# Units of 256 tokens by eight heads in a fused RWKV-6 and HyperMixer kernel: two tokens a partition, decay products on transposed operands, order from a list schedule

## Chip, cores, metric

One core of a Trainium2 chip. The time is device time of one execution in microseconds. Runs are marked fast or slow; on one core a run is called slow when it took over 1.5% more than the fastest of the same kernel. Comparisons below use fast runs unless the text says otherwise.

## The reference, cut

```python
# r, k, v, w: (4 batches, 8 heads, 768 tokens, 48); u: (8, 48)
for t in range(S):                                    # RWKV-6 with a decay of its own per channel
    cur = einsum('bhd,bhe->bhde', u * k[t], v[t])
    y[t] = einsum('bhd,bhde->bhe', r[t], state + cur)
    state = w[t][..., None] * state + einsum('bhd,bhe->bhde', k[t], v[t])
x = y as (4, 768, 384)                                # then a token MLP of each batch
wq, wk = x @ w_q, x @ w_k                             # 384 -> 64
mixed = (wq @ wk.T / 8) @ x
out = relu(mixed) @ w_out
```

Both kernels work in chunks of 128 tokens: within a chunk a masked product A of decayed r and k, across chunks a state SB of 48 x 48 a head; after that the MLP of a batch, which needs all its tokens. Decays are cumulated as logarithms with a triangular matmul (`cw`) and come back through Exp.

## The kernel before

Each of 16 preparations (`prep`) loads two heads over all 768 tokens of one batch. The decays go on in the natural layout, the products are transposed after that, and the diagonal term u*k*r is made in f32 on GpSimd and summed on VectorE. No order is given: the framework takes the program's.

```python
def prep(b, hp, AmB, RKT, VB, Vd, ptp):
    for ap, tl in ((w, wG), (k, kG), (r, rG), (v, vG)):
        nc.sync.dma_start(out=tl, in_=ap[b, ds(hp * 2, 2)].rearrange(
            "h (c p) d -> p (h c) d", p=C))               # packets of 192 bytes
    # ... Ln, two cw matmuls, Exp(+) to ecwx, Exp(-) to emcw ...
    nc.vector.tensor_tensor(pad(Rd), chd(rG), ecwx..., ALU.mult)
    nc.gpsimd.tensor_tensor(pad(Kd), chd(kG), emcw..., ALU.mult)     # KdS
    for c in range(NCH): mm(psT[:, 0, ds(c * C, C)], Rd[:, c], ID128, trans=True)
    for c in range(NCH): mm(psT[:, 1, ds(c * C, C)], Kd[:, c], ID128, trans=True)
    nc.vector.tensor_copy(RKT[:, hp], psT[:, :, 0:NCH * C])
    # ... A = K^T R by chunk, mask on VectorE ...
    nc.gpsimd.tensor_tensor(uk, hcd(kG), _rep(ubs, 2, NCH), ALU.mult)    # f32
    nc.gpsimd.tensor_tensor(uk, uk, hcd(rG), ALU.mult)                   # f32
    nc.vector.tensor_reduce(diag, uk, axis=AX.X, op=ALU.add)
    nc.gpsimd.tensor_tensor(Vd[...], VB[...], _rep(diag...), ALU.mult)

for b in range(B):
    for hp in range(NP): prep(b, hp, AmB, RKT, VB, Vd, ptp)
    # ... six chunks: Sn, SB, Y8, X, transposes of X; then the MLP ...
    for c in range(NCH):
        # ... fps matmuls ...
        nc.vector.tensor_copy(osb, fps)
        nc.sync.dma_start(out=out[b, ds(c * C, C), :], in_=osb)
```

Of the kernel before, what the change touches and what calls it, by code (L numbers as in the profile page):

```python
# [18 lines left out]
def _rep(ap, axis, n):  # L19
    a = [list(x) for x in ap.ap]  # L20
    a.insert(axis, [0, n])
    return dataclasses.replace(ap, ap=a)
# [3 lines left out]
def kernel(  # L26
# [14 lines left out]
    C = 128  # L41
    NCH = S // C
# [5 lines left out]
    scale = 1.0 / math.sqrt(DH)  # L48

    MU = -0.13468  # L50
    LN_SCALE = math.exp(-MU)

    def mm(o, l, rr, start=True, stop=True, sgc=True, trans=False):
        nc.tensor.matmul(o, l, rr, start=start, stop=stop,  # L54
                         skip_group_check=sgc, is_transpose=trans)
# [4 lines left out]
    U128 = consts.tile([C, C], BF16, tag="U128")  # L60
    make_upper_triangular(nc, U128, 1.0, diag=True)
    US128 = consts.tile([C, C], BF16, tag="US128")
    make_upper_triangular(nc, US128, 1.0, diag=False)
    ID128 = consts.tile([C, C], BF16, tag="ID128")
    make_identity(nc, ID128)
    ones = U128[:, C - 1:C]

    iota0 = consts.tile([C, 1], mybir.dt.int32, tag="iota0")
    nc.gpsimd.iota(iota0, pattern=[[0, 1]], base=0, channel_multiplier=1)
    iota1 = consts.tile([C, 1], mybir.dt.int32, tag="iota1")  # L70
    nc.gpsimd.iota(iota1, pattern=[[0, 1]], base=1, channel_multiplier=1)
    bias_px = consts.tile([C, 1], F32, tag="bpx")
    bias_mi = consts.tile([C, 1], F32, tag="bmi")
    bias_c = consts.tile([C, 1], F32, tag="bc")
    nc.scalar.activation(bias_px, iota0, ACT.Copy, bias=0.0, scale=MU)
    nc.scalar.activation(bias_mi, iota1, ACT.Copy, bias=0.0, scale=-MU)
    nc.gpsimd.memset(bias_c, MU * C)



    NB = 3
    LW = []
    RdS = []
    for i in range(NB):
        t = consts.tile([C, NCH, C], BF16, name=f"logw{i}", tag=f"logw{i}")
        nc.gpsimd.memset(t, 0.0)
        LW.append(t)
        t = consts.tile([C, NCH, C], BF16, name=f"RdS{i}", tag=f"RdS{i}")
        nc.gpsimd.memset(t, 0.0)
        RdS.append(t)  # L90
    KdS = []
    PT = []
    for i in range(2):
        t = consts.tile([C, NP, NCH, C], BF16, name=f"KdS{i}", tag=f"KdS{i}")
        nc.vector.memset(t, 0.0)
        KdS.append(t)
        t = consts.tile([C, NCH, H], F32, name=f"pt{i}", tag=f"pt{i}")
        nc.vector.memset(t, 0.0)
        PT.append(t)

    u1 = consts.tile([1, DM], F32, tag="u1")
    ubc = consts.tile([C, DM], F32, tag="ubc")
    wq_sb = consts.tile([128, NK, DH], BF16, tag="wq")
    wk_sb = consts.tile([128, NK, DH], BF16, tag="wk")
    wout_sb = consts.tile([128, NK, DM], BF16, tag="wo")
    wq_f = consts.tile([128, NK, DH], F32, tag="wqf")

    ld = ctx.enter_context(tc.tile_pool(name="ld", bufs=3))
    hw = ctx.enter_context(tc.tile_pool(name="hw", bufs=3))
    bt = ctx.enter_context(tc.tile_pool(name="bt", bufs=2))  # L110
    sm = ctx.enter_context(tc.tile_pool(name="sm", bufs=3))
    ps = ctx.enter_context(tc.tile_pool(name="ps", bufs=1, space=bass.MemoryType.PSUM))
    xpool = ctx.enter_context(tc.tile_pool(name="xpool", bufs=2))
    msb = ctx.enter_context(tc.tile_pool(name="msb", bufs=2))
    mout = ctx.enter_context(tc.tile_pool(name="mout", bufs=4))

    def mtile(shape, dtype, name):
        return ps.tile(shape, dtype, name=name, tag="m", bufs=2)

    def prep(b, hp, AmB, RKT, VB, Vd, ptp):  # L120
        n = b * NP + hp
        wG = ld.tile([C, 2 * NCH, D], F32, name="wG", tag="wG")
        kG = ld.tile([C, 2 * NCH, D], F32, name="kG", tag="kG")
        rG = ld.tile([C, 2 * NCH, D], F32, name="rG", tag="rG")
        vG = ld.tile([C, 2 * NCH, D], F32, name="vG", tag="vG")
        for ap, tl in ((w, wG), (k, kG), (r, rG), (v, vG)):
            nc.sync.dma_start(out=tl, in_=ap[b, ds(hp * 2, 2)].rearrange(  # L127
                "h (c p) d -> p (h c) d", p=C))
        if n == 0:
            nc.sync.dma_start(out=u1, in_=u.rearrange("h d -> (h d)"))  # L130
            nc.gpsimd.partition_broadcast(ubc, u1)

        def hcd(t):
            return t.rearrange("p (h c) d -> p h c d", h=2)

        def chd(t):
            return t.rearrange("p (h c) d -> p c h d", h=2)

        def pad(t):
            return t.rearrange("p c (h x) -> p c h x", h=2)[:, :, :, 0:D]  # L140

        logw = LW[n % NB]
        for hh in range(2):
            nc.scalar.activation(logw[:, :, ds(hh * 64, D)],  # L144
                                 wG[:, ds(hh * NCH, NCH)], ACT.Ln,
                                 bias=0.0, scale=LN_SCALE)
        cw1 = ps.tile([C, 2, 512], F32, name="cw1", tag="cw")
        for hh in range(2):
            mm(cw1[:, hh, 0:NCH * D], US128, logw[:, :, ds(hh * 64, D)])
        ecwx = hw.tile([C, 2, NCH, D], BF16, name="ecwx", tag="ecwx")  # L150
        nc.scalar.activation(ecwx.rearrange("p h c d -> p h (c d)"),  # L151
                             cw1[:, :, 0:NCH * D], ACT.Exp,
                             bias=bias_px, scale=1.0)
        cw0 = ps.tile([C, 2, 512], F32, name="cw0", tag="cw")
        for hh in range(2):
            mm(cw0[:, hh, 0:NCH * D], U128, logw[:, :, ds(hh * 64, D)])
        emcw = hw.tile([C, 2, NCH, D], BF16, name="emcw", tag="emcw")
        nc.scalar.activation(emcw.rearrange("p h c d -> p h (c d)"),  # L158
                             cw0[:, :, 0:NCH * D], ACT.Exp,
                             bias=bias_mi, scale=-1.0)  # L160
        for c in range(NCH):
            mm(ptp[:, hp, ds(c, 1)], logw[:, c], ones)

        Rd = RdS[n % NB]
        Kd = KdS[b % 2][:, hp]
        nc.vector.tensor_tensor(pad(Rd), chd(rG),  # L166
                                ecwx.rearrange("p h c d -> p c h d"), ALU.mult)
        nc.gpsimd.tensor_tensor(pad(Kd), chd(kG),  # L168
                                emcw.rearrange("p h c d -> p c h d"), ALU.mult)
        nc.scalar.copy(VB[:, :, ds(hp * 2, 2)], chd(vG))  # L170

        psT = ps.tile([C, 2, 1024], BF16, name="psT", tag="psT")
        for c in range(NCH):
            mm(psT[:, 0, ds(c * C, C)], Rd[:, c], ID128, trans=True)
        for c in range(NCH):
            mm(psT[:, 1, ds(c * C, C)], Kd[:, c], ID128, trans=True)
        nc.vector.tensor_copy(RKT[:, hp], psT[:, :, 0:NCH * C])  # L177

        NG = NCH // 2
        for g in range(2):  # L180
            A = ps.tile([C, 2, 512], F32, name="A", tag="A")
            for cc in range(NG):
                c = g * NG + cc
                for hh in range(2):
                    mm(A[:, hh, ds(cc * C, C)],
                       RKT[ds(hh * 64, D), hp, 1, ds(c * C, C)],
                       RKT[ds(hh * 64, D), hp, 0, ds(c * C, C)])
            nc.vector.tensor_tensor(  # L188
                AmB[:, ds(hp * 2, 2), ds(g * NG, NG)],
                A[:, :, 0:NG * C].rearrange("p h (c t) -> p h c t", c=NG),  # L190
                _rep(_rep(US128, 1, NG), 1, 2), ALU.mult)

        uk = hw.tile([C, 2, NCH, D], F32, name="uk", tag="uk")
        ubs = ubc[:, ds(hp * D2, D2)].rearrange("p (h d) -> p h d", h=2)
        nc.gpsimd.tensor_tensor(uk, hcd(kG), _rep(ubs, 2, NCH), ALU.mult)  # L195
        nc.gpsimd.tensor_tensor(uk, uk, hcd(rG), ALU.mult)  # L196
        diag = hw.tile([C, 2, NCH], F32, name="diag", tag="diag")
        nc.vector.tensor_reduce(diag, uk, axis=AX.X, op=ALU.add)
        nc.gpsimd.tensor_tensor(Vd[:, :, ds(hp * 2, 2)], VB[:, :, ds(hp * 2, 2)],  # L199
                                _rep(diag.rearrange("p h c -> p c h"), 3, D),  # L200
                                ALU.mult)

    for b in range(B):
# [6 lines left out]
        for hp in range(NP):  # L210
            prep(b, hp, AmB, RKT, VB, Vd, ptp)
# [16 lines left out]
        for c in range(NCH):  # L228
# [23 lines left out]
            if c + 1 < NCH:  # L252
                SB = SB2
# [74 lines left out]
```

## Time and profile before

182.25 us (median of 3, 181.02 to 184.86). The first part of the profile's page gives each engine's busy time and share of the span:

| | busy us before | share |
|---|---|---|
| TensorE (PE) | 121.0 | 66% |
| VectorE (DVE) | 112.7 | 62% |
| GpSimd (POOL) | 95.3 | 52% |
| ScalarE (ACT) | 74.0 | 41% |
| span | 182.1 | |

Such shares are averages over stages.

### The profile page before, as it was taken

What the parts mean: (1) busy time and instruction counts of PE and PEld (TensorE: products, weight loads), DVE (VectorE), ACT (ScalarE), POOL (GpSimd) and SP (SyncE); (2) the same over time, 40 slices, a digit from 0 to 9 for tenths busy, and PEclk for the clock granted to TensorE, in tenths of its full rate; (3) what the DMA queues carried; (4) which work ended last, traced back from release to release, by engine and by line L of the source; (5) the groups of instructions that cost most, each with busy time, mean ns of one, the idle gap of its engine ahead of it and who ended that gap; (6) DMA issues with size and microseconds to landing.
All of it is one profiled execution on the core that took longest, in us unless ns stands there. A gap on an engine that the chain in (4) does not pass through costs nothing.

```text
span 182.1 us, 3121 instructions
## 1 busy us (share of the span) xinstructions
PE 121.0 (66%) x1200; PEld 74.3 (41%) x1200; DVE 112.7 (62%) x156; ACT 74.0 (41%) x140; POOL 95.3 (52%) x86
## 2 busy tenths in 40 slices
PE   0152178130698787966988986688888964787791
PEld 0121045010465653343765533465564243565240
DVE  6011147469889977644799778179996553744042
ACT  3175473310045446066346461944456232022620
POOL 8410599999728976406993954379586202000000
PEclk9999999999999997585599999657999697557969
DMA  7999999999999300399999908999940240000024
GB/s 127 186 188 187 187 185 158 196 215 157 169 187 168 67 4 2 142 236 200 190 178 191 166 13 237 235 168 200 185 73 0 86 150 27 0 5 0 0 81 178
DMA packets 104000, 24.23 MB, mean 133 GB/s; under 512 B 100529, under 2 KB 103986, under 8 KB 103986
## 3 DMA queue, kind: packets, MB, share of 16 engines
q1 hardware_dynamic: 103186, 23.70, 76.7%
q0 software_dynamic: 800, 0.34, 1.5%
q8 instruction: 9, 0.15, 0.4%
q14 instruction: 5, 0.04, 0.1%
HBM read 19.66 MB, written 4.72 MB: 134 GB/s over the span
## 4 chain that ended last, share of the span: by engine, by line
PE 25%; DVE 23%; issue 18%; POOL 12%; ACT 7%; DMA 7%; SPq 6%; POOLq 1%; ACTq 0%; DVEq 0%
DVE RdS L166 6%; PE psT L54 6%; DVE X L250 5%; SPq L127 5%; DVE RKT L177 5%; POOL uk L196 4%; DMA wG<-in_w_dram 3%; ACT XT L260 3%; POOL uk L195 3%; PE cw L54 3%; POOL Vd L199 3%; PE wq_ps L54 2%; PE fps L54 2%; DVE AmB L188 2%; PE Tps L54 2%
## 5 line engine op out<-in xcount | busy, mean ns | idle before, releaser
L168 POOL TENSOR_TENSOR KdS<-kG,emcw 128x576 bf16<-128x576 f32 x16 | 22.2, 1388 | 41.5 <-ACT emcw L158 33.2
L188 DVE TENSOR_TENSOR AmB<-A,US 128x768 bf16<-128x768 f32 x32 | 30.4, 950 | 5.7 <-PE A L54 4.4
L166 DVE TENSOR_TENSOR RdS<-rG,ecwx 128x576 bf16<-128x576 f32 x16 | 20.8, 1298 | 20.2 <-ACT ecwx L151 14.6
L177 DVE COPY RKT<-psT 128x1536 bf16<-128x1536 bf16 x16 | 15.3, 953 | 19.4 <-PE psT L54 19.3
L195 POOL TENSOR_TENSOR uk<-kG,ubc 128x576 f32<-128x576 f32 x16 | 24.0, 1499 | 0.0
L196 POOL TENSOR_TENSOR uk<-uk,rG 128x576 f32<-128x576 f32 x16 | 23.6, 1476 | 0.6
L199 POOL TENSOR_TENSOR Vd<-VB,diag 128x576 bf16<-128x576 bf16 x16 | 18.7, 1172 | 8.4 <-ACT VB L170 6.2
L54 PE MATMUL A<-RKT 48*128 48x128 bf16 x192 | 17.5, 263 | 7.0 <-DVE RKT L177 4.2
L144 ACT ACTIVATE logw<-wG 128x288 bf16<-128x288 f32 x32 | 12.4, 435 | 23.7 <-PE ptp L54 11.3
L151 ACT ACTIVATE ecwx<-cw,bias_px 128x576 bf16<-128x576 f32 x16 | 11.9, 741 | 24.6 <-PE cw L54 24.5
L54 PEld LDWEIGHTS <-KdS 128*128 128x128 bf16 x176 | 16.1, 123 | 13.7 <-POOL KdS L168 9.9
L54 PEld LDWEIGHTS <-RKT 48*128 48x128 bf16 (+1 forms) x272 | 13.6, 108 | 19.6 <-issue 9.3
L54 PE MATMUL fps<-wout_sb,mixT 128*128 128x384 bf16 x72 | 19.7, 418 | 1.7 <-ACT mixT L288 1.2
L296 DVE COPY osb<-fps 128x384 f32<-128x384 f32 x24 | 13.0, 554 | 12.4 <-PE fps L54 12.2
L54 PE MATMUL cw<-logw,US 128*128 128x288 bf16 x32 | 10.5, 365 | 13.4 <-ACT logw L144 12.9
L260 ACT COPY XT<-xt_ps 128x768 bf16<-128x768 bf16 x12 | 9.6, 799 | 21.4 <-PE xt_ps L54 21.4
L158 ACT ACTIVATE emcw<-cw,bias_mi 128x576 bf16<-128x576 f32 x16 | 11.9, 742 | 11.3 <-PE cw L54 11.2
L54 PE MATMUL psT<-ID,RdS 128*128 128x128 bf16 x96 | 11.4, 272 | 7.5 <-DVE RdS L166 7.5
L54 PE MATMUL cw<-logw,U 128*128 128x288 bf16 x32 | 9.7, 386 | 8.4 <-ACT ecwx L151 8.4
L54 PE MATMUL psT<-ID,KdS 128*128 128x128 bf16 x96 | 12.7, 277 | 2.8 <-POOL KdS L168 2.8
L170 ACT CAST VB<-vG 128x576 bf16<-128x576 f32 x16 | 10.7, 666 | 7.8 <-DMA vG<-in_v_dram 7.7
L54 PE MATMUL Sn<-VB,KdS 128*128 128x96 bf16 x80 | 9.9, 238 | 5.4 <-POOL KdS L168 5.4
(53 smaller groups left out, 181.1 us busy)
## 6 DMA issues: line engine op xcount, KB each, us to landing
wG<-in_w_dram SPq DMA_DIRECT2D x16, 288.0 KB, 5.6
kG<-in_k_dram SPq DMA_DIRECT2D x16, 288.0 KB, 5.3
rG<-in_r_dram SPq DMA_DIRECT2D x16, 288.0 KB, 5.6
vG<-in_v_dram SPq DMA_DIRECT2D x16, 288.0 KB, 5.6
out_dram<-osb SPq DMA_DIRECT2D x24, 192.0 KB, 1.9
wout_sb<-in_moe_w_out_dram POOLq DMA_DIRECT2D x1, 288.0 KB, 4.8
wq_f<-in_moe_w_q_dram SPq DMA_DIRECT2D x1, 96.0 KB, 4.6
wk_sb<-in_moe_w_k_dram POOLq DMA_DIRECT2D x1, 48.0 KB, 4.6
```

Of the source, the lines that this page charges most:

```text
L54: nc.tensor.matmul(o, l, rr, start=start, stop=stop, skip_group_check=sgc, is_transpose=trans)
L144: nc.scalar.activation(logw[:, :, ds(hh * 64, D)], wG[:, ds(hh * NCH, NCH)], ACT.Ln, bias=0.0, scale=LN_SCALE)
L151: nc.scalar.activation(ecwx.rearrange("p h c d -> p h (c d)"), cw1[:, :, 0:NCH * D], ACT.Exp, bias=bias_px, scale=1.0)
L166: nc.vector.tensor_tensor(pad(Rd), chd(rG), ecwx.rearrange("p h c d -> p c h d"), ALU.mult)
L168: nc.gpsimd.tensor_tensor(pad(Kd), chd(kG), emcw.rearrange("p h c d -> p c h d"), ALU.mult)
L177: nc.vector.tensor_copy(RKT[:, hp], psT[:, :, 0:NCH * C])
L188: nc.vector.tensor_tensor(AmB[:, ds(hp * 2, 2), ds(g * NG, NG)], A[:, :, 0:NG * C].rearrange("p h (c t) -> p h c t", c=NG), _rep(_rep(US12 ...
L195: nc.gpsimd.tensor_tensor(uk, hcd(kG), _rep(ubs, 2, NCH), ALU.mult)
L196: nc.gpsimd.tensor_tensor(uk, uk, hcd(rG), ALU.mult)
L199: nc.gpsimd.tensor_tensor(Vd[:, :, ds(hp * 2, 2)], VB[:, :, ds(hp * 2, 2)], _rep(diag.rearrange("p h c -> p c h"), 3, D), ALU.mult)
L260: nc.scalar.copy(XT[:, :, ds((c - 1) * C, 2 * C)], tp)
L296: nc.vector.tensor_copy(osb, fps)
```

## The change

The intent: fewer and larger instructions, larger packets, no f32 products, and an order that interleaves work instead of leaving it to the program text. There are now 12 units (4 batches of 3), each of 256 tokens and all heads. r and k are cast, transposed raw, and multiplied by the decays in PSUM's transposed layout; u*k*r becomes a matmul of `qT` with u. Every step is put into a plan with an engine, an estimated duration, its predecessors and the buffers that it takes and gives. A list scheduler then emits the steps in the order in which its own simulated clock starts them, so **the plan's clock decides each engine's program order, and the chip has to keep it**.

```diff
+class Plan:
+    def add(self, eng, dur, rank, fn, after=(), take=(), give=(), lag=0): ...
+    def order(self):       # at each simulated time: start the ready step of lowest rank whose
+        ...                # engine and buffers are free; a step is over for those that
+        return done        # follow it after dur + lag
...
+    plan = Plan({"w": 3, "s": 2, "ld": NB, "lw": 2, "rk": 2, "ep": 2, "x": 2})
...
+        lw_ = add("SP", 1500, R, lambda: load(b, i, wg, w), state["ld"], take=["ld"], lag=2000)
+        lr_ = add("SP", 1500, R, lambda: load(b, i, rg, r), [lw_], lag=2000)
+        lk_ = add("SP", 1500, R, lambda: load(b, i, kg, k), [lr_], lag=2000)
+        lv0 = add("SP", 1100, R, lambda: load_v(b, i, vg, 0), [lk_], lag=2000)
+        lv1 = add("SP", 1100, R, lambda: load_v(b, i, vg, 1), [lv0], lag=2000)
+        state["ld"] = [lv1]
+        ln = add("ACT", 860, R + 10, f_ln, [lw_], take=["lw"])
+        r16_ = add("POOL", 950, R + 10, f_c16(r16, rg), [lr_], take=["rk"])
...
+        rT = add("PE", 460, R + 12, f_rawT("rT", r16), [r16_], take=["s"], lag=150)
+        qT = add("DVE", 700, R + 13, f_qT, [rT, ks])            # rT in PSUM times ks
+        vb = add("POOL", 950, R + 18, f_vb, [lv0, lv1])
...
+    with tc.manual_schedule():
+        for s in plan.order():
+            s["fn"]()
-            nc.gpsimd.tensor_tensor(uk, hcd(kG), _rep(ubs, 2, NCH), ALU.mult)
-            nc.gpsimd.tensor_tensor(uk, uk, hcd(rG), ALU.mult)
-            nc.vector.tensor_reduce(diag, uk, axis=AX.X, op=ALU.add)
```

Tags: "w" are PSUM buffers of two banks (3 of them), "s" of one bank (2 of them). The stores remain on the queue of the loads (SP).

Names in the traces, in the order of a unit: `lw` is Ln of w, `cw` its sums, `ep` and `en` are Exp of +cw and -cw; `rT` and `kT` the raw transposes, `ks` the copy of kT, `qT` = rT x ks; `RT` and `KT` are r and k with their decays; `dps` and `dd` the u*k*r term; `VB` is v scaled, `Vd` VB times dd; `A` and `AM` the product within a chunk before and after the mask; `kb` and `KD` KT transposed back; `sn` and `SB` the state, `ptm` its decay; `y` and `X` the result of the recurrence, `xt` and `XT` X transposed. Of the MLP are `qk` and `QK`, `T` and `TS`, `mx` and `MX`, `fp` and `os`.

## The prediction

> **What bounds the kernel now.** I read the page first (busy shares, slices, chain), then the waits, then windows and the timeline. The first view is the page: busy time per engine, then the slices and the chain.
>
> ```profile
> span 182.1 us, 3121 instructions
> PE 121.0 (66%) x1200; PEld 74.3 (41%) x1200; DVE 112.7 (62%) x156; ACT 74.0 (41%) x140; POOL 95.3 (52%) x86
> ...
> DMA  7999999999999300399999908999940240000024
> ...
> PE 25%; DVE 23%; issue 18%; POOL 12%; ACT 7%; DMA 7%; SPq 6%; POOLq 1%; ACTq 0%; DVEq 0%
> ```
>
> No engine is above 66% busy, DMA is full early and empty for long stretches later, and the chain changes engine all the time. So the limit is dependence between engines, not one engine. The waits and GpSimd's timeline show where:
>
> ```profile
> POOL KdS L168 <- ACT emcw L158: 33.2, 10, 8.4
> ...
> SPq L297 <- DVE osb L296: 66.4, 19, 25.7
> ...
> 82.50 1.27 POOL L168 TENSOR_TENSOR KdS<-kG,emcw 128x576 bf16<-128x576 f32 x1 [7.51 <-ACT emcw L158]
> ...
> 116.85 1.28 POOL L168 TENSOR_TENSOR KdS<-kG,emcw 128x576 bf16<-128x576 f32 x1 [5.33 <-ACT emcw L158]
> ...
> 151.42 1.27 POOL L168 TENSOR_TENSOR KdS<-kG,emcw 128x576 bf16<-128x576 f32 x1 [8.39 <-ACT emcw L158]
> ```
>
> The queue that issues the loads stood behind output stores for 66.4 us, so a batch's last loads wait for the previous batch's end. The same step of three batches starts at 82.50, 116.85 and 151.42: **one batch costs 34.4 us**, although preparation of the next batch overlaps the MLP of the last. That is the number to beat.
>
> Durations that I reuse (groups by shape: count | total, mean ns) and TensorE at two speeds (timeline):
>
> ```profile
> L188 DVE TENSOR_TENSOR AmB<-A,US 128x768 bf16<-128x768 f32 x32 | 30.4, 950 | 5.7 <-PE A L54 4.4 <-PE mps L54 1.0
> L177 DVE COPY RKT<-psT 128x1536 bf16<-128x1536 bf16 x16 | 15.3, 953 | 19.4 <-PE psT L54 19.3
> L238 DVE TENSOR_TENSOR SB<-Sn,pt 128x384 bf16<-128x384 f32 x20 | 11.0, 548 | 2.6 <-PE Sn L54 2.5
> L158 ACT ACTIVATE emcw<-cw,bias_mi 128x576 bf16<-128x576 f32 x16 | 11.9, 742 | 11.3 <-PE cw L54 11.2
> L260 ACT COPY XT<-xt_ps 128x768 bf16<-128x768 bf16 x12 | 9.6, 799 | 21.4 <-PE xt_ps L54 21.4
> L86 POOL MEMSET logw<- 128x768 bf16 x3 | 2.2, 738 | 0.0
> ...
> 150.90 0.51 PE L54 MATMUL psT<-ID,RdS 128*128 128x128 bf16 x6
> 158.20 0.96 PE L54 MATMUL xt_ps<-ID,X 128*128 128x128 bf16 x6 [0.68 <-DVE X L250]
> ```
>
> **What the Trainium skill says.** (1) "TensorE: Matmul & The Clock Gate", Part 1: the array runs at half clock unless kept active. The trace agrees: six transposes take 0.51 us or 0.96 us, and its start-to-start times are 56 or 107 ns for a transpose and 162 or 320 ns for 384 columns. Its specification table says that ScalarE, VectorE and GpSimd queues are strict FIFO, and Part 2 that only weight loads are pulled ahead. So program order is binding; the argument below rests on it. (2) "VectorE: DVE Perf Modes", The perf-mode tier table: a tensor_tensor with a PSUM operand runs at one element a cycle; Why PSUM operands drop a tier caps PSUM at the packed two-element mode and only fp32 at one. The trace shows a bf16 PSUM copy at two (1536 in 953 ns), an fp32 PSUM tensor_tensor at one (768 in 950 ns), and no bf16 PSUM tensor_tensor. This stays open. (3) "ScalarE: Activation LUTs", What ACT_TABLE_LOAD costs: 186 ns + 0.833 ns an element, some 93 ns more for each per-partition operand. The trace has 799 for 768 elements (826 by the formula) and 742 for 576 with a bias (759): near enough.
>
> **The change, by engine sums.** There are now 12 units of 256 tokens and 8 heads. DVE per unit: the k copy, qT, RT and KT at 0.69 each (1024 at two a cycle is 533, plus the 153 fixed of the 1536 copy: 953 - 800), two masks at 1.22 (1024 / 0.96 + 150), two SB at 0.55, XT 0.55, 0.17 for the diagonal; with one SB in 12 units fewer per batch, 6.8 us. ACT by the formula: Ln 0.83, two Exp of 1024 at 1.04, KD 0.90 (mean), X 0.89 to 0.92, QK 0.5, and a third of a batch's T copy, three ReLU and three output copies, 1.8: 7.0 us. GpSimd: two casts, V scaled, Vd: 4.7. DMA: w, r and k come in 384-byte packets instead of 192, 5120 packets a unit. The packet records show 16 ns for 192 bytes and 65 for the 1536-byte writes, so a line through both gives 23 for 384 (an estimate); (3072 x 23 + 2048 x 16 + 256 x 65) / 16 = 7.5 us. Removed: the f32 u*k*r products on GpSimd (24.0 + 23.6 us) and the 11.9 us of reduction on DVE. TensorE at full clock is about 6.4. **Sums alone would say 12 x 7 to 8 plus start and end, 120 to 130 us.**
>
> **What the order does to that.** The order listing of the built program shows that almost nothing of that overlaps. The plan makes each load wait in its own clock for the load before it with 2 us of landing, 3 x 3.5 + 2 x 3.1 = 16.7 us a unit. It therefore believes that r and k of the next unit come when this unit is finished, and writes that into every engine's order. TensorE's order is y(n), cw(n+1), xt(n), qk(n), rT(n+1), kT(n+1), dps, A0, A1, kb, sn0, sn1, y(n+1); GpSimd casts r only after ptm, which needs Exp of that unit, behind X(n) on ACT. The chip does not wait so for loads, but it keeps the order. The walk, from the start of X(n) on ACT at full clock, with 0.04 us a hop as in the trace: X 0.9; Exp behind it to 1.9; ptm, r cast, k cast (0.95 each: 1-input, near the memset's 738) to 4.0. Beside it xt, XT, qk end by 2.8 to 2.9. Eight transposes of k, 0.45 + 0.2, to 4.7; the DVE row ks, qT, RT, KT 4 x 0.69 to 7.4; A0 0.5 to 8.0; two masks to 10.4; SB0 0.55; sn1 0.33; y (two times 162 + 8 x 25 + 4 x 42) 1.06 + 0.2 to 12.7. Back-to-back DVE overlaps of some 0.08 bring it to **12.4 us a unit**; half clock adds 2.6 (k transposes late by 1.1, A0 0.1, sn1 0.3, y 1.1).
>
> At a batch's first unit, ACT must do T copy, three ReLU and three output copies before KD, and TensorE T, mx, fp before A0: QK to 3.5, T 4.5, TS 5.0, mx 5.4, ReLU to 7.8, fp0 to fp2 to 10.8, A0 11.4, masks 13.9, y's second half after SB0 and sn1, 15.4: **15.3 us**, plus about 5 at half clock. The second unit has Ln behind X, before Exp: 1.4 more than the plain one, **13.8**.
>
> Sum with 40% of the time at half clock: plain 13.4, first 17.3, second 14.8, a batch 45.5 against 34.4 now. Start to X(0): weights are loaded before r and cast before it, k cast at 10.9, transposes 11.6, plus 8.0 from there: 20.5 with a cold array. Then 2 x 13.4 = 26.8 and 3 x 45.5 = 136.5. After the last X: 11.8 to the last output copy as above, 2.5 to store, 1.7 half clock: 16. **Total 20.5 + 26.8 + 136.5 + 16 = 200 us.**
>
> **Rivals.** (A) Units overlap after all, engine sums rule: near 125 us. For it: all sums fall, the plan's slots allow three loads ahead. Against: the order leaves no next-unit work before qk(n). (B) TensorE stays at full clock: 12.4, 15.3, 13.8 in the same sum are 20 + 24.8 + 124.5 + 14.5 = 184 us, about the same as now. Against: TensorE has idle stretches of 2 to 3 us in each unit, like the last 40 us of the trace, where the granted clock was 0.73 to 0.78. (C) qT and RT run at one element a cycle: 1.22 instead of 0.69, 1.05 a unit, 12 to 13 us more, 212. (D) DMA bounds: 7.5 us a unit lies below 12.4, so loads are hidden; only the start shows them.
>
> **Range and chances.** 184 (B) to 218 (C, with a little more half clock). The walk would have to be 11% too long for a gain of over 2%; I give that 0.1, because the author's own durations give much the same chain. Within 2% needs B complete: 0.14. Slower: 0.76.
>
> **What would show it.** Right: X starts 12 to 15 us apart and 15 to 20 at a batch's start; DMA share well under full; ks(n+1) on DVE starts after XT(n) with idle time ended by TensorE; ACT under 50% busy, TensorE, DVE and GpSimd likewise. C is read from the mean of qT and RT (690 or 1220). Wrong: X starts 8 to 9 us apart, any engine near 85%, or ks(n+1) waiting on loads.

## The result and the profile after

206.8 us (median of 4, 205.45 to 210.67) against 182.29 us (4 runs, 181.02 to 184.86): ratio 1.140, 95% interval 1.123 to 1.158, slower. Ratios here compare fast runs of the same rounds, so they are not quite the ratio of the medians (the means of the fast runs for this pair give 1.135). The profiled run is a fast one of 205.76 us.

From the page of the kernel after: busy times, granted clock and DMA in 40 slices, and the chain by engine.

```profile
span 204.1 us, 3589 instructions
PE 127.2 (62%) x1480; PEld 89.4 (44%) x1480; DVE 81.6 (40%) x131; ACT 81.3 (40%) x103; POOL 70.2 (34%) x79
...
PEclk9999985965799555787995555976999555585599
DMA  6999890000039899300049999200059980000016
...
PE 33%; issue 24%; DVE 14%; SPq 9%; ACT 8%; POOL 7%; DMA 1%; POOLq 0%; ACTq 0%; DVEq 0%
```

The arithmetic did shrink: VectorE by 31 us, GpSimd by 25 us. None of it shortened the run. DMA is under a tenth busy in 16 of 40 slices, and no engine but TensorE is above 40%. The waits (engine, line, what it waited for: total us, times, longest) name the hand-overs:

```profile
POOL ptm L312 <- ACT ep L269: 78.3, 11, 9.1
ACT KD L370 <- PE kb L124: 54.8, 12, 8.3
DVE ks L290 <- PE kT L124: 53.0, 12, 7.4
...
ACT lw L244 <- DMA wg<-in_w_dram: 8.6, 4, 2.5
```

`ptm`, `KD` and `ks` wait 11 or 12 times, once a unit: all units wait at the same three places, so one unit is gone through after the other. The windows from one start of X on ScalarE to the next give the time a unit takes (columns: window, us, busy us of PE, PEld, DVE, ACT, POOL with counts, granted clock, DMA share, GB/s):

```profile
21.60:35.53 13.93, 9.03 (x122) 6.53 (x120) 6.69 (x10) 5.08 (x7) 5.42 (x5) 0.77 0.62 142
35.53:47.30 11.77, 7.91 (x113) 5.81 (x113) 6.05 (x9) 4.61 (x6) 5.42 (x5) 0.79 0.00 0
47.30:63.49 16.19, 13.29 (x143) 8.71 (x141) 6.75 (x10) 9.44 (x12) 5.42 (x5) 0.82 0.25 69
63.49:82.78 19.29, 10.60 (x122) 7.99 (x124) 6.72 (x11) 5.95 (x8) 5.44 (x5) 0.58 1.02 246
82.78:94.39 11.61, 7.75 (x113) 5.62 (x113) 6.04 (x9) 4.64 (x6) 5.42 (x5) 0.81 0.05 9
94.39:109.67 15.28, 11.83 (x143) 7.67 (x141) 6.77 (x10) 9.32 (x13) 5.42 (x5) 0.93 0.30 77
109.67:127.84 18.17, 10.91 (x122) 8.20 (x124) 6.70 (x10) 5.94 (x7) 5.44 (x5) 0.50 1.08 256
```

In a unit of 11.6 us each of VectorE, ScalarE and GpSimd has only 4.6 to 6.0 us of work, and TensorE 7.8 at a granted clock of 0.81: the sum of hand-overs is what is paid. From 47.30 a batch is the sum of three such rows: 47.1 us for the first, and 45.2 and 46.4 for the others (X starts at 94.39, 109.67, 127.84, 139.63, 154.49, 173.41 and 186.05), where the kernel before took 34.4.

One row is odd. The second unit of a batch takes 18 to 19 us where the same kind of unit at 21.60, in the first batch, took 13.93. Its start in time order (start us, duration us, in brackets idle time before it), first the queue of SP, then ScalarE:

```profile
57.83 4.00 SPq L513 DMA_DIRECT2D out_dram<-os  x6
61.88 0.60 SPq L159 DMA_DIRECT2D wg<-in_w_dram  x1
...
63.49 0.90 ACT L422 ACTIVATE X<-y,gx 128x768 bf16<-128x768 f32 x1 [2.18 <-PE y L124]
66.86 0.84 ACT L244 ACTIVATE lw<-wg 128x768 bf16<-128x768 f32 x1 [2.46 <-DMA wg<-in_w_dram]
```

The load of w for this unit stands in the queue behind the six output stores of the batch before; it is issued at 61.88 and Ln can start only at 66.86. In the three such units Ln waited 2.46, 1.35 and 2.32 us for w (the fourth wait of the line above, 2.49 us, is that of the first unit of all). Here Ln also comes behind X in ScalarE's own order, where in the first batch it comes before X, as the prediction says of a second unit. The DMA digits show the same thing: idle for some 25 us ahead of it, although unit 1, whose buffers these loads take over, had its X done at 36.4, then full.

Three groups by shape (count | total us, mean ns | idle before) settle two sizes of the prediction:

```profile
L294 DVE TENSOR_TENSOR qT<-rT,ks 128x1024 bf16<-128x1024 bf16 x12 | 8.3, 692 | 0.4
L298 DVE TENSOR_TENSOR RT<-rT,ep 128x1024 bf16<-128x1024 bf16 x12 | 8.2, 681 | 0.0
L319 POOL TENSOR_SCALAR VB<-vg,gv 128x768 bf16<-128x768 f32 x12 | 26.5, 2205 | 3.1 <-DMA vg<-in_v_dram 3.0
```

`qT` and `RT` with their bf16 operand in PSUM go at two elements a cycle (1024 in 0.69 us; at one they would take the 1.22 us of the masks). `VB` takes 2.2 us where the plan and I had 0.95.

The order listing of the built programs, with matmuls of one step taken together, shows what "one unit after the other" means for TensorE. It is no profile but the program itself; "after" is from its second unit on, the other line is the kernel of the first experiment:

```
after              cw xt qk rT kT dps A0 A1 kb sn0 sn1 y | cw xt qk rT kT dps A0 A1 kb sn0 y | ...
e1_plan_landing    dps cw dps sn0 rT sn1 y y xt qk xt cw qk kT rT dps A0 A1 kb cw sn0 y kT y rT xt A0 A1 qk ...
```

### The profile page after: what moved, and what is told of

Its sections match the earlier page's. It is cut to its first block, busy times and chain, and to the rows that moved or that the text cites. A ratio compares the mean times of both kernels' runs of the same rounds, so it can differ in the third digit from the quotient of the medians.

```text
span 204.1 us, 3589 instructions
## 1 busy us (share of the span) xinstructions
PE 127.2 (62%) x1480; PEld 89.4 (44%) x1480; DVE 81.6 (40%) x131; ACT 81.3 (40%) x103; POOL 70.2 (34%) x79
## 4 chain that ended last, share of the span: by engine, by line
PE 33%; issue 24%; DVE 14%; SPq 9%; ACT 8%; POOL 7%; DMA 1%; POOLq 0%; ACTq 0%; DVEq 0%
PE y L124 6%; PE fp L124 5%; SPq L166 5%; ACT MX L489 4%; POOL Vd L335 4%; SPq L159 4%; PE qk L124 3%; PE T L124 3%; PE kT L124 3%; DVE ks L290 3%; DVE qT L294 3%; DVE KT L305 2%; DVE RT L298 2%; PE A L124 2%; PE rT L124 2%
## 5 line engine op out<-in xcount | busy, mean ns | idle before, releaser
L370 ACT COPY KD<-kb 128x1024 bf16<-128x1024 bf16 (+1 forms) x12 | 10.4, 870 | 54.8 <-PE kb L124 54.8
L354 DVE TENSOR_TENSOR AM<-A,US 128x1024 bf16<-128x1024 f32 x24 | 28.3, 1220 | 5.4 <-PE A L124 5.4
L312 POOL TENSOR_TENSOR ptm<-ep,MB 128x16 f32<-128x16 bf16 x12 | 2.6, 217 | 78.3 <-ACT ep L269 78.3
L319 POOL TENSOR_SCALAR VB<-vg,gv 128x768 bf16<-128x768 f32 x12 | 26.5, 2205 | 3.1 <-DMA vg<-in_v_dram 3.0
L335 POOL TENSOR_TENSOR Vd<-VB,dd 128x768 bf16<-128x768 bf16 x12 | 17.7, 1475 | 27.4 <-DVE dd L331 27.4
L124 PE MATMUL cw<-CM,lw 64*128 64x128 bf16 x192 | 11.4, 289 | 12.3 <-ACT lw L244 12.3
L124 PEld LDWEIGHTS <-KT 48*128 48x128 bf16 (+1 forms) x272 | 13.6, 117 | 10.2 <-DVE KT L305 8.3
L124 PE MATMUL fp<-wo,MX 128*128 128x384 bf16 x72 | 13.8, 328 | 3.4 <-ACT MX L489 3.3
L124 PEld LDWEIGHTS <-KD 128*128 128x128 bf16 x80 | 6.2, 122 | 20.6 <-ACT KD L370 14.1
L392 DVE TENSOR_TENSOR SB<-sn,ptm 128x384 bf16<-128x384 f32 x20 | 11.1, 556 | 10.0 <-PE sn L124 10.0
L269 ACT ACTIVATE ep<-cw 128x1024 bf16<-128x1024 f32 x12 | 12.5, 1041 | 4.8 <-PE cw L124 4.3
L124 PEld LDWEIGHTS <-AM 128*128 128x128 bf16 x192 | 12.1, 118 | 4.1 <-issue 3.3
L244 ACT ACTIVATE lw<-wg 128x768 bf16<-128x768 f32 x12 | 10.1, 845 | 8.6 <-DMA wg<-in_w_dram 8.6
L124 PE MATMUL y<-VB,AM 128*128 128x48 bf16 x192 | 12.4, 211 | 0.2 <-DVE AM L354 0.2
```

What stands on the lines that cost most here:

```text
L124: nc.tensor.matmul(o, l, rr, start=start, stop=stop, skip_group_check=True, is_transpose=trans)
L244: nc.scalar.activation(view(lw, 0, [[64, H], [512, 2], [1, D]]), view(wg, 0, [[D2, H], [D, 2], [1, D]]), ACT.Ln, bias=0.0, scale=math.exp( ...
L269: nc.scalar.activation(view(ep, 66, [[EW, 8], [-65, 2], [1, 64]]), t["cw"], ACT.Exp, bias=0.0, scale=1.0)
L319: nc.gpsimd.tensor_scalar_mul(sb("VB", [C, 2 * DM]), vg[:, ds(0, 2 * DM)], gv)
L335: nc.gpsimd.tensor_tensor(sb("Vd", [C, 2 * DM]), t["VB"], view(t["dd"], 0, [[1, 2 * H], [0, D]]), ALU.mult)
L354: nc.vector.tensor_tensor(view(sb(f"AM{g}", [C, 1024]), 0, [[C, 8], [1, C]]), view(t[f"A{g}"], 0, [[C, 8], [1, C]]), view(US, 0, [[0, 8], ...
```

## Experiments

The first theory is the prediction's: the chain of landings in the plan's clock writes a serial order. The second theory is for the odd unit: the load behind the stores. Rivals: the buffers (PSUM above all) make it serial whatever the plan believes, and the granted clock is the cause and not a companion. All kernels gave the right result.

### e1_plan_landing: loads follow each other's issue in the plan

```diff
-        lw_ = add("SP", 1500, R, lambda: load(b, i, wg, w), state["ld"], take=["ld"], lag=2000)
-        lr_ = add("SP", 1500, R, lambda: load(b, i, rg, r), [lw_], lag=2000)
+        def issue(name, dur, fn, before, take=()):
+            one = add("SP", dur, R, fn, before, take=take)
+            return one, add(f"land {name} {n}", 2000, R, lambda: None, [one])
+        iw, lw_ = issue("w", 1500, lambda: load(b, i, wg, w), state["ld"], take=["ld"])
+        ir, lr_ = issue("r", 1500, lambda: load(b, i, rg, r), [iw])
...                                    # k, v0, v1 alike
```

No instruction is added or removed; only their order is another.

> One thing is changed in the plan, nothing in the instructions: a load follows the load before it on the queue when that one is issued (1.5 us), instead of when it has landed (3.5 us), so the plan believes 6.7 us a unit instead of 16.7. The emitted order then interleaves two units on TensorE, VectorE and GpSimd. Theory (the serial order written by the plan's slow loads made the kernel 206 us): X starts 8 to 10.5 us apart instead of 12 to 19, total 135 to 160 us. Rival 1 (the new unit of work itself is dear: TensorE at half clock, GpSimd's 2.2 us V scaling, real loads): the order matters little, 195 to 207 us. Rival 2 (PSUM slots bind even so): 165 to 185 us.

174.67 us (173.0 to 176.51), ratio to before 0.962 (0.948 to 0.976). Mean of the fast runs 174.1 against 206.3 for the kernel after, so the order was worth 32 us, the higher granted clock that came with it (0.84 instead of 0.764) included. Page and waits of this kernel:

```profile
span 172.7 us, 3598 instructions
PE 116.7 (68%) x1480; PEld 86.5 (50%) x1480; DVE 81.9 (47%) x131; ACT 79.3 (46%) x103; POOL 71.3 (41%) x79
...
ACT KD L374 <- PE kb L124: 28.5, 9, 5.2
...
DVE ks L294 <- PE kT L124: 22.3, 12, 4.7
```

The waits of KD and ks are halved. That of ptm for ep (78.3 us) is down to 3.4, but part of it has only moved to `VB` on the same engine (see e10). Theory confirmed for its direction; its size (135 to 160, X 8 to 10.5 us apart) was missed: X starts 11.5 us apart on average, and the time fell into the range of the rival with the PSUM buffers. Something else still held the units.

### e2_stores_act: the stores leave the queue of the loads

```diff
             def f_os(ii=ii, osb=osb):
                 nc.scalar.copy(view(osb, 0, ...), view(t[f"fp{ii}"], 0, ...))
+                f_st(ii, osb)
...
-                    nc.sync.dma_start(
+                    nc.scalar.dma_start(
                         out=dst[j], in_=view(osb, 0, [[DM, 2], [1, DM]], p0=64 * j, pn=64))
-            add("SP", 1000, R + 42 + ii, f_st, [os_], lag=2000)
```

> The order of the changed kernel on all compute engines is kept; only its output stores leave the queue that issues the loads and go to ACT's, right behind the copy that they store. Theory (the second unit of each batch took 18 to 19 us instead of my 14.8 because its w load stood behind the stores of the batch before): the second unit falls to 14 to 15.5 us, the wait of Ln for the w load goes away, total 193 to 198 us. Rival (w is late for another reason, such as DMA bandwidth or the buffer of three units): second unit stays at 18 to 19 us, total 205 to 208 us.

210.23 us (203.71 to 212.25); only the 203.71 was a fast run, and the profiled one (208.37) was not. That one run lies 1.3% under the 206.3 of the kernel after and in neither expected range: no clear gain. The edit also does more than its expectation says: without the store steps the plan comes to another order. Replaying the two plans shows it: on ScalarE Ln of a batch's second unit has moved from behind X of the first to before it (and on TensorE cw before xt). So this run takes the stores from ahead of the load and Ln from the path behind X, both at once.

The second units fell as the theory wanted, from 19.3, 18.2 and 18.9 us to 13.5, 15.2 and 15.2, and the first batch's second unit, with no store ahead of it in either kernel, took 13.4 (13.9 before). The two effects together were worth some 4 us a batch; the waits for w that are gone were 2.0 us of it on average, the rest is not taken apart. But the first units of a batch rose from 15 to 16 us to 18.7, 20.8 and 20.6 (at granted clocks of 0.86, 0.75 and 0.75 instead of 0.82, 0.93 and 0.93, so the rise need not be ScalarE's alone). ScalarE of this kernel at that place (ACTq: time in which it issues):

```profile
55.83 1.35 ACTq L508 DMA_DIRECT2D out_dram<-os  x2
57.22 0.80 ACT L512 COPY os<-fp 128x768 f32<-128x768 f32 x1 [1.42 <-PE dps L124]
58.05 1.36 ACTq L508 DMA_DIRECT2D out_dram<-os  x2
59.46 0.80 ACT L512 COPY os<-fp 128x768 f32<-128x768 f32 x1 [1.44 <-PE kb L124]
60.28 1.26 ACTq L508 DMA_DIRECT2D out_dram<-os  x2
61.59 1.01 ACT L370 COPY KD<-kb 128x1024 bf16<-128x1024 bf16 x1 [1.33 <-issue]
62.50 0.85 ACT L244 ACTIVATE lw<-wg 128x768 bf16<-128x768 f32 x1
65.67 0.90 ACT L422 ACTIVATE X<-y,gx 128x768 bf16<-128x768 f32 x1 [2.33 <-PE y L124]
```

Three pairs of stores hold ScalarE for 1.35 + 1.36 + 1.26 = 4.0 us, and KD, which the state update needs, stands behind them; Ln (`lw`) now stands in this unit too. The wait was not removed but handed to an engine on the path.

### e3_both: e1 and e2 together

> Both edits together. If head-of-line blocking also matters in the pipelined order, the gain over the first run alone is 5 to 12 us (130 to 150 us); if the loads are far enough ahead there, within 2 us of the first run, or some us slower because ACT issues the stores.

182.65 us (180.35 to 184.12), ratio to before 1.001 (0.981 to 1.020). The fast runs (181.1 on average) are 7 us behind those of e1 in the same rounds: with interleaved units there was little left to win from the loads (Ln's waits for w are 7.4 us here and 10.1 in e1), while in the chain that ended last ScalarE's issuing takes 7% of the span. That the issuing is the whole of the 7 us is not shown; the profiled run was a slow one, and the order of Vd on GpSimd differs a little too.

### b1_stores_act: the kernel before with its stores on ScalarE's queue

```diff
-            nc.sync.dma_start(out=out[b, ds(c * C, C), :], in_=osb)
+            nc.scalar.dma_start(out=out[b, ds(c * C, C), :], in_=osb)
```

> The kernel before, with its 24 output stores issued from ACT's queue instead of the loads' queue. If the 66 us that its load queue stood behind stores set the batch period of 34.4 us, 165 to 178 us. If the loads had slack, 180 to 184 us. If ACT now waits for the output copies of VectorE in its own order, slower, 184 to 192 us.

184.12 us (183.46 to 184.75), ratio 1.017 (1.007 to 1.027): no gain, and by the 2% rule not clearly a loss. The 66.4 us that SP waited behind stores in the kernel before, which the prediction reads as delaying a batch, could not be turned into time this way. The start of a batch's Ln on ScalarE, first in the kernel before, then in this one:

```profile
78.81 1.11 ACT L144 ACTIVATE logw<-wG 128x288 bf16<-128x288 f32 x3 [7.12 <-issue]
...
78.88 1.11 ACT L144 ACTIVATE logw<-wG 128x288 bf16<-128x288 f32 x3 [6.60 <-DMA out_dram<-osb]
```

Ln starts at the same time in both. In the kernel before the profile names no load as what ended its wait there, and at the same place of the next two batches for TensorE's ptp (5.33 and 5.98 us). So Ln was not held by its load there; in this kernel the stores on ScalarE's queue fill the same gap.

### e4_warm: matmuls into unread columns to keep TensorE's clock up

```diff
+            for m in range(WARM):                 # 5, behind dps
+                mm(x[:, ds(128, 384)], t["qT"][:, ds(0, C)], t["ks"][:, ds(0, 384)])
...
+                        for m in range(WARM2):    # 8, behind sn0
+                            mm(x[:, ds(384, 128)], t["KT"][:, ds(0, C)], t["RT"][:, ds(0, 128)])
```

> The changed kernel in its own order, with dummy matmuls on real data in two places where TensorE waits (five of 384 columns behind dps, eight of 128 behind sn0, into columns that nobody reads). They test my rival B, the clock. If the low clock (0.764) costs what I summed, 2.2 to 2.6 us in a plain unit, and the dummies keep the clock up (0.85 or more), the time falls to 192 to 200 us. If the clock does not rise, or the dummies themselves lie on the path, 205 to 212 us.

216.04 us (211.26 to 218.15; the 211.26 alone fast, within the 205 to 212 for dummies that lie on the path). The mean clock rose from 0.764 to 0.826 in the profiled run, but the added matmuls, in the middle of the chain, cost more than that gave. This misses as a test: it doesn't say what a full clock alone would be worth in the kernel after. A hint stands in e2's trace: its second units, all with the same order, took 13.42, 13.52, 15.20 and 15.20 us at granted clocks of 0.82, 0.75, 0.50 and 0.50.

### e5_named_slots: e1 with three edits to the plan

(1) Each PSUM tile gets the buffer that the plan chose instead of the next of a pool; (2) three SBUF buffers of each tile and a limit of three units in flight; (3) measured durations, among them:

```diff
-        return ps.tile([C, 1024 if dtype == F32 else 2048], dtype, name=name, tag="w", bufs=3)
+        return ps.tile([C, 1024 if dtype == F32 else 2048], dtype, name=name, tag=f"w{at['w']}", bufs=1)
-        def sb(name, shape, dtype=BF16, bufs=2):
+        def sb(name, shape, dtype=BF16, bufs=3):
-        vb = add("POOL", 950, R + 18, f_vb, [lv0, lv1])
+        vb = add("POOL", 2200, R + 18, f_vb, [lv0, lv1])
-        cw = add("PE", 500, R + 11, f_cw, [ln], take=["w"], give=["lw"], lag=150)
+        cw = add("PE", 600, R + 11, f_cw, [ln], take=["w"], give=["lw"], lag=200)
```

> On top of the first run: the plan names the PSUM buffer that each tile gets (before, the pool handed buffers out in turn, which the plan did not know), SBUF tiles have three buffers, and the plan has durations as measured. PSUM is still three buffers of two banks and two of one. Theory (first run fell short of 135 to 160 us because the two one-bank buffers bind, not because the plan was inaccurate): 168 to 176 us. Rival (buffers in turn and wrong durations, GpSimd's 2.2 us most of all, threw the order off): 150 to 162 us.

162.29 us (160.74 to 163.69), ratio 0.885 (0.878 to 0.893): 12 us less than e1. The theory (168 to 176) is refuted, the rival about right in size. Which of the three edits did it is taken apart below.

### e6_four_small: e5 with PSUM as two large and four small buffers

```diff
-    plan = Plan({"w": 3, "s": 2, "ld": NB, "lw": 2, "rk": 2, "ep": 2, "x": 3})
+    plan = Plan({"w": 2, "s": 4, "ld": NB, "lw": 2, "rk": 2, "ep": 2, "x": 3})
```

> The run e5_named_slots with PSUM split as two buffers of two banks and four of one, the same eight banks. Theory (one-bank buffers bind): 145 to 156 us, X 8.5 to 10 us apart. Rival (accuracy of the plan, the clock or GpSimd bind): within 4 us of e5_named_slots.

**133.54 us** (133.1 to 134.52), ratio 0.735 (0.730 to 0.741). This beats both kernels, and my range (145 to 156); X starts 8.0 us apart on average (8.5 to 10 expected). Its page:

```profile
span 131.6 us, 3582 instructions
PE 100.3 (76%) x1480; PEld 74.0 (56%) x1480; DVE 78.9 (60%) x131; ACT 79.3 (60%) x103; POOL 71.8 (55%) x79
...
PEclk9999997799999999999999999965899999976998
DMA  3999999999998995889978989999850084000075
```

The work is the same 1480 matmuls and 131 VectorE instructions as in the kernel after; TensorE's busy time fell from 127.2 to 100.3 us because its clock was granted at 0.945 instead of 0.764. A unit uses rT, kT, dps, kb, sn, xt and qk in small buffers, and with two of them a tile must wait until another is read out; that these waits are the 29 us is argued from the edit, since the plan also writes another order for the new split. DMA is now nearly full from the second slice to the 28th but for two or three slices: the DMA engines are the likely next bound, which no run tests.

### e7_landing_back: e6 with only the landing chain put back

The five `add` lines of the change in place of `issue`, nothing else.

> The run e6_four_small with only the plan's waits of each load for the landing of the load before put back. Theory (these waits alone make the order serial, whatever the buffers): 196 to 210 us. Rival (with enough PSUM buffers the landing waits matter less): 165 to 185 us.

212.31 us (206.16 to 213.6; the 206.16 alone fast). Against e6 (133.7, mean of its runs in the same rounds) that is 72 us by five lines that only the plan reads. TensorE's order is the kernel after's again but for small swaps, and so are the DMA digits:

```profile
DMA  6999990000009899400019799600019980000026
```

VectorE's order is the kernel after's exactly. With e1 this settles the cause from both sides: with the landing chain the kernel is serial with either split of PSUM, without it the buffers and the durations decide how far units interleave.

### e8, e9, e10: the three edits of e5, one at a time on e1

> The kernel of e1_plan_landing with one of the three edits that made e5_named_slots of it: each PSUM tile is given the buffer that the plan chose for it, so that a tile no longer waits for a buffer that the plan did not mean. Theory (the 12 us between 174.7 and 162.3 are waits for PSUM buffers of the wrong tile): 161 to 166 us. Rival (they come from the durations in the plan): 171 to 177 us, since the durations are those of e1_plan_landing.

> The kernel of e1_plan_landing with measured durations in the plan alone (VB 2.2 instead of 0.95 us, PE steps about a quarter longer, casts 0.83). Theory of named buffers: 170 to 177 us, near e1_plan_landing. Rival (the durations decide, since the plan puts VB ahead of what it then holds up): 161 to 167 us.

> The kernel of e1_plan_landing with three instead of two SBUF buffers of each tile of a unit and a limit of three units in flight in the plan; the order of instructions on each engine is unchanged by it. In e1_plan_landing VB waits 10.4 us for ks and 6.6 us for y, which are waits for a buffer that has its earlier reader still to come. If those waits set the time: 163 to 169 us. If, as I rather think, GpSimd's waits lie beside the path: 172 to 176 us.

Run together on one chip, 3 rounds:

| kernel | median us (range) | ratio to before (95%) |
|---|---|---|
| e8_named_only | 174.41 (172.94 to 175.52) | 0.953 (0.945 to 0.960) |
| e9_durations_only | 162.55 (159.23 to 164.42) | 0.878 (0.868 to 0.889) |
| e10_sbuf_three | 174.95 (173.93 to 175.81) | 0.958 (0.951 to 0.965) |

The durations alone are the whole step from e1's 174.7 to e5's 162.3; the naming of PSUM buffers is worth nothing by itself, nor are the SBUF buffers. The replayed plans agree: e9 and e5 have the same order on every engine, and so have e1, e8 and e10. So e1's waits of VB on GpSimd (10.4 us for ks, 6.6 us for y) lay beside the path, as that expectation leaned: in e10 they are gone, and ptm's wait for ep is 31.3 us instead of e1's 3.4. GpSimd's idle time had only changed its place. Which of the durations matters most (VB was off by 1.25 us, the PE steps by some 100 ns each) was not taken apart.

### e11_three_of_each: e6 with a third buffer of lw, r, k and the exponentials

> The kernel of e6_four_small with three instead of two buffers of the decay logarithm, of the casts of r and k and of the exponentials, in SBUF and in the plan. If e6_four_small is still held by units starting late, 126 to 131 us; if it is held by the tensor engine (76% busy) and its hand-overs within a unit, which these buffers do not touch, 132 to 136 us. I hold the second to be likelier.

137.63 us (136.46 to 138.84), ratio 0.752 (0.746 to 0.758): slower than e6's 0.735, and just outside my range. More depth isn't free: the plan's own estimate had fallen by 1 us (134.9 to 133.8). Whether units starting late hold e6 stays open, because the edit hardly moved their starts (Ln of the third to the seventh unit at 20.4, 30.4, 36.4, 42.0 and 49.4 us, in e6 at 19.6, 31.3, 36.8, 42.5 and 50.0).

## Why the prediction was right, and which term was off

**The direction and its cause were right.** The serial order was read from the built program before any run, e1 and e7 show that the landing chain makes it, and the shape of the trace is the predicted one: ks of the next unit stands behind TensorE's kT (53.0 us of idle time), ptm behind Exp (78.3), DMA is idle in stretches. Rival A (units overlap, near 125 us) failed for this kernel, and e6's 133.5 shows that the instructions themselves can do it. Rival C (qT and RT at one element a cycle) is refuted by 692 and 681 ns. Rival D's claim that the loads are hidden held for most units but not for the second of a batch, see below. Rival B (full clock, 184) did not come about; e4 didn't isolate it.

**The sum, term by term** (measured: starts of X in the profiled run):

| term | predicted | measured |
|---|---|---|
| start to X(0) | 20.5 | 21.6 |
| two units of the first batch | 2 x 13.4 = 26.8 | 13.93 + 11.77 = 25.7 |
| first unit of a batch | 3 x 17.3 = 51.9 | 16.19 + 15.28 + 14.86 = 46.3 |
| second unit | 3 x 14.8 = 44.4 | 19.29 + 18.17 + 18.92 = 56.4 |
| third unit | 3 x 13.4 = 40.2 | 11.61 + 11.79 + 12.64 = 36.0 |
| after the last X | 16.0 | 18.05 |
| sum, the span | 199.8 | 204.1 |
| span to time | left out | 205.76 - 204.1 = 1.7 |

- *Second unit*: 12 us too little in all, 4 a unit, and this is the step that failed. "DMA bounds: 7.5 us a unit lies below 12.4, so loads are hidden" compared rates and forgot the queue: the load waits for its turn behind six stores, not for bandwidth. Ln's waits for w (2.46, 1.35 and 2.32) are 6.1 of the 12 us. By the prediction's own 2.6 us for half clock all the way, the granted clocks of 0.58, 0.50 and 0.62 instead of 0.8 are 3.6 more (an estimate). Of the remaining 2.2, some 1.3 is that Ln and cw put Exp off by 1.7 to 1.9 us beside the wait and not by 1.4; the rest is unexplained. The unit of the first batch (13.93) is no full twin, since its Ln comes before X; nor does e2 show the predicted 14.8, since it has Ln before X too.
- *First unit*: 5.6 us too much. Half of it is the clock: granted were 0.82, 0.93 and 0.93 instead of the 0.8 that 40% of half clock means. With these clocks the walk gives 17.1, 16.0 and 16.0, still 0.7 to 1.1 us a unit too much. A share of half clock spread evenly over the units was a wrong model: the low clock gathers in the second ones.
- *Third unit*: 4.2 us too much. At the assumed clock (0.79 to 0.81) these took 11.6 to 11.8 instead of 13.4. A batch's last unit has one state update fewer, which I took off VectorE's sum and not off the walk. A unit with both updates and no stores ahead (21.60) took 13.93. These two errors nearly cancel the first: that the total of 200 comes so near is luck.
- *Tail*: the last output copy ended 12.6 us after X (11.8 predicted); the stores took 5.4 instead of 2.5, since six of them are issued one after the other in 3.99 us.
- *What would show it*: X 12 to 15 us apart held roughly for plain units (11.6 to 13.9); "15 to 20 at a batch's start" held for the first and, unforeseen, for the second. ACT (40%), DVE (40%) and POOL (34%) are under 50% busy as said, TensorE with 62% is not.
- *The step on the kernel before*: SP's 66.4 us behind stores was read as holding up batches; b1 doesn't confirm it, and the starts of Ln shown there speak against it.

**Where the expected gain went.** The change saves 56 us of VectorE and GpSimd work, but in the plan's clock a chain of landings that doesn't exist on the chip (its queue issues the next load after 0.6 us) set the order, so the saved work became idle time.

**What stays open**: what the clock alone is worth in the kernel after; how much of e6's last 29 us is the buffers on the chip and how much the order that the plan makes of them, as they change together (the plan's own estimate falls by 22 us, from 156.9 to 134.9); and whether DMA bounds e6.

## What to carry to other kernels

When a scheduler writes the order, its model is part of the kernel: read the order that it built, check each duration against a trace, and let a transfer's landing delay its readers but never the next issue. Judge a prefetch by its place in the queue as well as by bandwidth, and before moving stores to another queue look at what stands behind them on the engine that will issue them. Where the same hand-over waits in every unit and no engine is near full, count the buffers of the small intermediate tiles: trading one PSUM buffer of two banks for two of one bank, with the order that the plan made of it, took 29 us off here, where the 56 us of removed engine work had taken off nothing by themselves.

## What the Trainium skill lacked or had wrong

- "VectorE: DVE Perf Modes", The perf-mode tier table: its entry for a tensor_tensor with any PSUM operand (one element a cycle) is wrong for bf16. `qT` with rT in PSUM took 692 ns and `RT` 681 ns for 1024 elements, as against 1220 ns for the masks with an fp32 PSUM operand. The page's own later section, Why PSUM operands drop a tier, has it right.
- "GPSIMD Engine Reference", 4.1 Engine selection, says that one-input work on GpSimd goes roughly at line rate. True of the casts (768 elements, fp32 to bf16, 825 and 829 ns), not of a tensor_scalar with a per-partition operand from SBUF: the same 768 elements took 2205 ns, more than the two-input Vd (1475 ns).
- "DMA: Bandwidth & Descriptors", Issuing engines are not separate DMA queues, calls the issue time that a second engine saves usually small. It lacks the cost to that engine: two stores held ScalarE for 1.26 to 1.36 us in the batch shown, 4.0 us ahead of KD, and e3 with this issuing took 7 us more than e1.
- No page spells out that a load placed behind stores that still wait for their data waits with them: w, issued at 61.88 us after a store block of 4.00 us, made Ln idle for 2.46 us, and for 1.35 and 2.32 us in the next two batches.
